# A spectral filter stage with its outer frequencies moved from the free dimension to the partitions

## The chip, the core and the metric

The kernel runs on one core of a Trainium2 chip. The metric is the device time of one execution in microseconds (us), the median of several runs. The profile is one execution of the same program, taken by the hardware profiler.

## The reference

One block of a diffusion-like network over a sequence of 2048 tokens with 640 features, in bf16. A conditioning row `c` gives six modulation vectors (shift, scale and gate for each of two halves). The first half filters the normalised input with a global spectral filter; the second half is a gated feed-forward network.

```python
mod = (silu(c) @ w_mod).reshape(1, 6, 1, 640)
sa, ca, ga, sb, cb, gb = (mod[:, i] for i in range(6))
h = layernorm(x) * (1 + ca) + sa                 # x: (1, 2048, 640)
X = rfft2(h)                                     # (2048, 321) complex
y = irfft2(X * (w_r + 1j * w_i))                 # w_r, w_i: (2048, 321)
x = x + ga * y
h = layernorm(x) * (1 + cb) + sb
x = x + gb * ((silu(h @ w_gate) * (h @ w_up)) @ w_down)   # 640 -> 1728 -> 640
```

Nothing in the reference depends on data: the Fourier transforms can be written as products with constant tables.

## The kernel before

Each token has a number 16 p + t, with p on the 128 partitions and t the tile (16 tiles). The order of instructions on every engine is the order of the calls in the source; each engine (TensorE as PE, VectorE as DVE, ScalarE as ACT, GpSimd as POOL, the DMA queue of SyncE as SP) runs its own in that order and waits on semaphores. Every DMA issued on SP or ACT uses one of eight semaphores in turn, so a DMA is issued only after the one eight places earlier has landed.

**Loads.** SP loads x, the scale columns of w_mod (`wm_ca`), the tables R and G, then (among the last x tiles and the shift columns `wm_sa`) the filter. Two `flip` DMAs (L267) copy w_i and w_r through DRAM into `wflip`, rows reversed; two small edge copies each go on POOL's queue (L261, L263). Two loads (L277) bring the unflipped filter into `Wn`, and two (L426) bring the flipped one from `wflip` into `Wv`; both have the inner row number k1 on the 128 partitions and 256 of the 321 columns. The remaining four column blocks of w_mod (`wm_r`: gate of the first half, then shift, scale and gate of the second) are loaded in two places: the first block ahead of the filter's last loads (L279), the other three behind the transposes (L527, L528).

**Tile loop (L466).** For each tile, PE transposes x (`t1`, L335), ACT copies it (L338), a product with R gives the feature transform (`dfwd`, L315 and L318), DVE corrects it by the mean (`zout`, L382), and `s1` (L393, L394) multiplies with G, scaled on POOL by the reciprocal deviation (`gscale`), for the inner part of the token transform. ACT writes the result to `A_sb` (L397; the last tile in three pieces, L400). The mean and variance of a tile come either from `bn` on DVE (the tiles named in `BN`) or from `gram_stats` (a product on PE and two DVE instructions). Tiles 9 to 15 are handled with reversed token order (`FLIP`). `wsum` (L407) forms w_r + w_i for a three-product complex multiplication, in slices spread over DVE and POOL.

**Filter stage (L516 to L731).** The 321 feature frequencies are four images of 81 base columns l, worked in 21 groups of up to four columns. The first five groups are transposed on PE (`t2_pe`), the others by four DMA transposes (`t2_dma`, L519), so that tile, complex part and residue (16 x 2 x 4) are on the partitions. `stage_a` (L567) multiplies each column, as the weights, with the table KS2: the result in PSUM has the inner frequency k1 on the partitions and 192 outer values (three products x 16 outer frequencies x 4 images) along the free dimension. `prod` (L592) multiplies them with the filter on DVE, 2 instructions of 128x384 per group. `stage_b` (L599) multiplies each of the two halves of the product with the identity: this sums and transposes back, with the outer frequencies on the partitions; ACT copies the result to `Y2` (L602). `stage_c` (L620) applies the inverse outer transform from Ktab; `evac` (L632 to L637) copies two groups at a time to `Em` or `Er`, and `rot` (L648, POOL mostly) writes their rotated copies. The 15 products of `mod_col` (L580, 5 instructions each) for the shift, scale and gate columns of the second half stand near the stage's end. POOL adds the shift's transform `SA` to the transposed columns (`sa_add`, L559).

**The rest.** The inverse transforms (`s1em` L669, `s1er` L678, L1184, L1187), the second normalisation, and the feed-forward network in four chunks follow (L1013, L1043, L891, L914). Its weights are loaded into the filter's buffer once the last filter product is done (`load_gu`, L746).

Of the kernel before, what the change touches and what calls it, by code (L numbers as in the profile page):

```python
# [20 lines left out]
NW = 256  # L21
# [3 lines left out]
BN = (0, 1, 4, 8, 14)  # L25
# [18 lines left out]
def _tables():  # L44
# [39 lines left out]
    KS2 = np.zeros((16, 2, 4, 3, 2, 16, 2))  # L84
    KI = np.zeros((3, 2, 2, 16, 2, 16, 4, 2))
    for m in range(4):
        hl, mm = m // 2, m % 2
        k2 = q if hl == 0 else 15 - q
        F16 = np.exp(-2j * np.pi * np.outer(q, k2) / 16)
        for r in range(4):  # L90
            M = real2(F16 * (-1j) ** (m * r))
            if hl:
                M[:, 1] *= -1
            M = M.transpose(2, 0, 1, 3)
            KS2[:, :, r, 1, hl, :, mm] = M[:, :, 0]
            KS2[:, :, r, 0, hl, :, mm] = -M[:, :, 0] - M[:, :, 1]
            KS2[:, :, r, 2, hl, :, mm] = M[:, :, 1] - M[:, :, 0]
            f = (1.0, 1j ** r, (-1.0) ** r, (-1j) ** r)[m]
            for v in range(3):
                M = real2(F16.conj().T * f * (np.exp(1j * np.pi * r / 4) if v == 2 else 1.0))  # L100
                if hl:
                    M[1] *= -1
                if v >= 1:
                    M[:, 1] *= -1
                KI[v, hl, :, :, mm, :, r, :] = M.transpose(0, 2, 3, 1)
    K = np.zeros((128, 3 * 128 + 192))
    for v in range(3):
        K[:, 128 * v:128 * v + 128] = KI[v].transpose(1, 0, 2, 3, 4, 5, 6).reshape(128, 128)
    K[:, 384:] = KS2.reshape(128, 192)
# [46 lines left out]
def adaln_block_kernel(ctx, tc, A_x, A_w_r, A_w_i, B_x, B_w_gate, B_w_up, B_w_down, c, w_mod, out):  # L156
# [25 lines left out]
    Ktab = const.tile([P, 576], BF16, name="Ktab")  # L182
    KS2 = Ktab[:, 384:576]
# [31 lines left out]
    Wn = rW.cut(0, [3, NT, NW])  # L215
    Wv = rW.cut(24576, [3, NT, NW])
# [39 lines left out]
    dram = ctx.enter_context(tc.tile_pool(name="dram", bufs=1, space=bass.MemoryType.DRAM))  # L256
    Wflip = [dram.tile([P, NT, NW], BF16, name=n) for n in ("wflip_i", "wflip_r")]

    def flip_edge(w, f):
        ncol = w.ap[0][0]  # L260
        nc.gpsimd.dma_start(f[0:1, 0:NT - 1, :], bass.AP(tensor=w.tensor, offset=w.offset + P * ncol + 65,  # L261
                                                        ap=[[P * NT * ncol, 1], [P * ncol, NT - 1], [1, NW]]))
        nc.gpsimd.dma_start(f[0:1, NT - 1, :], w[0:1, 65:65 + NW])  # L263

    def flip(w, f):
        ncol = w.ap[0][0]
        nc.sync.dma_start(f[1:P].rearrange("p k l -> k p l"),  # L267
                          bass.AP(tensor=w.tensor, offset=w.offset + 127 * ncol + 65,
                                  ap=[[P * ncol, NT], [-ncol, P - 1], [1, NW]]))

    nc.sync.dma_start(x_sb[:, 8:12, :], x_v[:, 8:12, :])
    flip(A_w_i, Wflip[0])
    nc.sync.dma_start(x_sb[:, 12:16, :], x_v[:, 12:16, :])  # L273
    flip(A_w_r, Wflip[1])
    nc.sync.dma_start(wm_sa[:], wm_v[:, :, 0:D])  # L275
    for i, w in ((0, A_w_i), (2, A_w_r)):
        nc.sync.dma_start(Wn[:, i, :, :], w.rearrange("(k2 k1) l -> k1 k2 l", k1=P)[:, :, 0:NW])  # L277
    wm_m = wm_v[:, :, 2 * D:6 * D].rearrange("p k (i d) -> p k i d", i=4)
    nc.sync.dma_start(wm_r[:, :, 0, :], wm_m[:, :, 0, :])  # L279
    nc.sync.dma_start(KS2, K_dram[:, 384:576])  # L280
# [44 lines left out]
    if True:  # L325
# [76 lines left out]
        def wsum(W, lo, hi, eng):  # L402

            off = lo if W is Wn else NW - hi
            v = [_rev(W, NT * NW * i + off, [[NW, NT], [160, 2], [1, hi - lo]]) if W is Wn else
                 _rev(W, NT * NW * i + off - 160, [[NW, NT], [160, 2], [1, hi - lo]]) for i in range(3)]
            eng.tensor_tensor(v[1], v[2], v[0], ALU.add)  # L407
# [15 lines left out]
        flip_edge(A_w_i, Wflip[0])  # L423
        flip_edge(A_w_r, Wflip[1])
        for i in range(2):
            nc.sync.dma_start(Wv[:, 2 * i, :, :], Wflip[i][:])  # L426
        nc.sync.dma_start(Ktab[:, 0:384], K_dram[:, 0:384])
# [38 lines left out]
        for t in range(2, NT + 2):  # L466
# [33 lines left out]
            if t in (13, 15):  # L500
                if t == 13:
                    wsum(Wn, 48, 64, nc.vector)
                else:
                    wsum(Wn, 0, 48, nc.vector)
# [7 lines left out]
    if True:  # L512
# [12 lines left out]
        t2_dma(2)  # L525
        t2_dma(3)
        nc.sync.dma_start(wm_r[:, :, 1:3, :], wm_m[:, :, 1:3, :])  # L527
        nc.sync.dma_start(wm_r[:, :, 3, :], wm_m[:, :, 3, :])  # L528
        nc.sync.dma_start(Htab[:], H_dram)
# [23 lines left out]
        def sa_add(g):  # L553
# [3 lines left out]
            if l0 not in seen:  # L557
                seen.add(l0)
                nc.gpsimd.tensor_tensor(B2b[:, :nb, 0:1], B2b[:, :nb, 0:1], SA[:, l0:l0 + nb].unsqueeze(2), ALU.add)  # L559

        def stage_a(g):
            ls = groups[g]
            n = len(ls)
            xps = banks(6 if g == 2 else 2 + 2 * (g % 2), 2, [4, 256])
            for i, l in enumerate(ls):
                B2, j = B2of[l][0:2]
                nc.tensor.matmul(xps[:, i, 0:192], lhsT=B2[:, j, :], rhs=KS2, start=True, stop=True)  # L567
                if i == 0:
                    for c5 in {NG - 4: (0, 1), NG - 3: (0, 1), NG - 2: (2, 3, 4), NG - 1: (2, 3, 4)}.get(g, ()):
                        mod_col(psum[:, 2 + 2 * (g % 2), 192 + c5:193 + c5], wm_r[:, :, 1 + g % 2], c5)  # L570
            PP = rM.cut(1536 * (g % 4), [3, 2, NT, 2, n])
            prod(g, PP, xps, 0)
            if g == 0:
                wsum(Wv, 48, 64, nc.vector)
            prod(g, PP, xps, 1)
# [7 lines left out]
        def prod(g, PP, xps, hl):  # L583
            ls = groups[g]
            n = len(ls)
            xv = xps[:, :n, 0:192].rearrange("p i (v h k m) -> p v h k m i", v=3, h=2, k=NT)
            st = ls[1] - ls[0]
            if hl == 0:
                in1 = _rev(Wn, ls[0], [[NT * NW, 3], [NW, NT], [160, 2], [st, n]])
            else:  # L590
                in1 = _rev(Wv, 255 - ls[0], [[NT * NW, 3], [NW, NT], [-160, 2], [-st, n]])
            nc.vector.tensor_tensor(PP[:, :, hl], xv[:, :, hl], in1, ALU.mult)  # L592

        def stage_b(g, PP):
            n = len(groups[g])
            yps = banks((g + 1) % 2, 1, [4, 128])
            for ps in (1, 0):
                for i in range(n):
                    nc.tensor.matmul(yps[:, i, :], lhsT=_rev(PP, 64 * n * ps + i, [[n, 128]]), rhs=identb[:],  # L599
                                     start=(ps == 1 and i == 0), stop=(ps == 0 and i == n - 1))  # L600
            Y2 = rY.cut(1024 * (g % 4), [4, 128])
            nc.scalar.copy(Y2[:, 0:n, :], yps[:, 0:n, :])  # L602
            return Y2

# [5 lines left out]
        units = [(0, 1), (2, 3), (4,)] + [(g, g + 1) for g in range(5, NG - 2, 2)] + [(NG - 2,), (NG - 1,)]  # L610

        def stage_c(u):
            for g in units[u]:
                ls = groups[g]
                n, l0 = len(ls), ls[0]
                eps_ = banks({NG - 4: 4, NG - 3: 5, NG - 2: 0, NG - 1: 1}.get(g, 6 + (l0 // 4) % 2), 1, [4, 128])
                Y2 = Y2s.pop(g)
                for i, l in enumerate(ls):
                    kv = {0: 1, 80: 2}.get(l, 0)
                    nc.tensor.matmul(eps_[:, i + 4 - n if l0 else i, :], lhsT=Y2[:, i, :], rhs=Ktab[:, 128 * kv:128 * kv + 128],  # L620
                                     start=True, stop=True)

        def evac(u):
            g, l0 = units[u][0], groups[units[u][0]][0]
            if l0 == 0:
                edge = rY.cut(4096, [2, 128])
                nc.scalar.copy(edge[:], banks(6, 1, [4, 128])[:, 0:2, :])
# [3 lines left out]
            elif g == NG - 2:  # L631
                nc.vector.tensor_copy(ep_views(l0, 4), banks(0, 1, [4, 128]).rearrange("p i q -> p q i"))  # L632
            elif g == NG - 1:
                nc.scalar.copy(ep_views(l0, 4), banks(1, 1, [4, 128]).rearrange("p i q -> p q i"))
            else:
                n = len(groups[g]) + 4
                (nc.vector.tensor_copy if g == NG - 6 else nc.scalar.copy)(  # L637
                    ep_views(l0, n), banks(4 if g == NG - 4 else 6, 2, [8, 128])[:, 8 - n:8, :].rearrange("p i q -> p q i"))
                if g < NG - 4:
                    rots.extend((l0, n, i) for i in range(0 if g == NG - 6 else 2))  # L640
# [21 lines left out]
        def s1b(t):  # L662
            return 6 if t == 1 else 2 if t == 0 or t % 2 else 4
# [18 lines left out]
        PPs, Y2s, rots = {}, {}, []  # L682
        ga_mod(320, 5, range(3))
        t2_pe(0)
        t2_pe(1)
        ga_mod(320, 5, range(3, NC5))
        PPs[0] = stage_a(0)
        t2_pe(2)
        t2_pe(3)
        wsum(Wn, 80, 81, nc.gpsimd)  # L690
        PPs[1] = stage_a(1)
        ga_mod(0, 0)
        PPs[2] = stage_a(2)
        for g in range(NG + 1):
# [627 lines left out]
```

## Time and profile before

| | us |
|---|---|
| runs (3) | 249.75, 250.11, 250.72; median 250.11 |
| profiled execution: span from the first to the last instruction | 247.5 (its time outside the span is not on the page) |
| busy in the span: PE / DVE / ACT / POOL | 241.6 / 208.2 / 167.6 / 77.9 |
| filter stage, first transposes to the first L669 product | about 37 to 63 |
| mean DMA rate over the span | 140 GB/s; 281 to 407 GB/s in every 2 us window but one (262) from 4 to 38 us |

In rows of instruction groups the columns are line, engine, operation, output<-input with shapes, count, then busy us and mean ns of one, then the idle time of the engine just before them and what ended it. A line number is that of the kernel before. The granted TensorE clock is 1.00 in every stretch.

### The profile page before, as it was taken

Reading aid. Unit: us, or ns where it says so; the run is one execution under the profiler, and the core shown is the slowest. Engines: PE = TensorE matmul, PEld = TensorE weight load, DVE = VectorE, ACT = ScalarE, POOL = GpSimd, SP = SyncE. Lnnn points to the kernel's source line nnn. Section 1 sums busy time; section 2 is a strip of 40 time slices with the busy share of each in tenths; the row PEclk is TensorE's granted clock in tenths of the full one; section 3 lists DMA queues with packets and bytes.
Section 4 is the critical chain, followed back from the end, with each engine's and each line's share of the span. In section 5 each row is a group of like instructions: output and inputs, shape, how many; then the busy total and the mean of one; then the engine's idle time right before and its main releaser. Section 6 shows DMA issues by size and latency. Waiting matters only on the chain.

```text
span 247.5 us, 6172 instructions
## 1 busy us (share of the span) xinstructions
PE 241.6 (98%) x2327; PEld 189.3 (76%) x2327; DVE 208.2 (84%) x516; ACT 167.6 (68%) x327; POOL 77.9 (31%) x128
## 2 busy tenths in 40 slices
PE   8999998999999999999999999999999999999994
PEld 3778876999999888688887778887765566656773
DVE  4799887998899998789989977788998787789864
ACT  3778756897989698489774488766246777773220
POOL 8577764895243514002004400000432000004400
PEclk9999999999999999999999999999999999999999
DMA  6999999999999999500005110200411000000111
GB/s 211 399 357 301 288 381 219 189 353 390 307 345 304 291 283 191 128 15 3 0 3 106 53 56 3 54 3 19 93 50 53 3 0 1 4 0 0 53 56 53
DMA packets 45759, 34.74 MB, mean 140 GB/s; under 512 B 21731, under 2 KB 42658, under 8 KB 45346
## 3 DMA queue, kind: packets, MB, share of 16 engines
q1 hardware_dynamic: 43936, 30.00, 43.0%
q0 software_dynamic: 1504, 4.28, 7.3%
q8 instruction: 18, 0.29, 0.5%
q10 hardware_dynamic: 290, 0.08, 0.2%
q14 instruction: 11, 0.09, 0.1%
HBM read 27.05 MB, written 4.72 MB: 128 GB/s over the span
## 4 chain that ended last, share of the span: by engine, by line
PE 81%; SPq 10%; DMA 6%; DVE 1%; issue 1%; ACT 0%; DVEq 0%; ACTq 0%
PE psum L1043 36%; PE psum L914 19%; PE psum L1013 6%; DMA rW<-wflip_r 4%; PE psum L599 3%; PE psum L891 3%; PE psum L669 3%; PE psum L567 2%; SPq L273 2%; SPq L277 2%; SPq L275 2%; DMA rM<-in_w_mod_dram 2%; PE psum L620 2%; PE psum L1184 2%; SPq L279 2%; PE psum L1187 2%
## 5 line engine op out<-in xcount | busy, mean ns | idle before, releaser
L1043 PEld LDWEIGHTS <-rW 128*128 128x128 bf16 (+1 forms) x429 | 41.9, 98 | 12.7
L1043 PE MATMUL psum<-rW 128*128 128x256 bf16 (+1 forms) x247 | 42.2, 287 | 0.0
L940 POOL TENSOR_TENSOR rM<-rM,rL 128x320 f32<-128x320 f32 x6 | 5.4, 907 | 96.6 <-ACT rL L939 96.6
L914 PEld LDWEIGHTS <-rE 128*128 128x128 f16 (+1 forms) x196 | 19.0, 97 | 7.8
L914 PE MATMUL psum<-rE 128*128 128x320 f16 (+1 forms) x147 | 22.9, 299 | 0.0
L592 DVE TENSOR_TENSOR rM<-psum,rW 128x384 bf16<-128x384 f32 (+2 forms) x42 | 20.1, 543 | 2.0 <-PE psum L567 1.4
L1074 ACT COPY rH<-psum 128x384 f32<-128x384 f32 (+2 forms) x27 | 13.9, 516 | 7.4 <-PE psum L1043 6.0
L1081 ACT COPY rX<-psum 128x384 f32<-128x384 f32 (+2 forms) x27 | 14.0, 519 | 7.3 <-PE psum L1043 7.0
L1043 PEld LDWEIGHTS <-rE 128*128 128x128 f16 x156 | 15.2, 98 | 4.7
L1078 DVE TENSOR_TENSOR rH<-psum,rM 128x512 bf16<-128x512 f32 (+1 forms) x24 | 15.0, 624 | 4.4 <-PE psum L1043 2.2
L1097 ACT ACTIVATE rL<-psum 128x384 bf16<-128x384 f32 (+2 forms) x27 | 14.4, 532 | 5.3 <-PE psum L1043 3.4
L1082 DVE TENSOR_TENSOR rX<-psum,rX 128x384 f32<-128x384 f32 (+2 forms) x27 | 16.3, 604 | 1.6 <-ACT rX L1081 1.4
L1068 ACT COPY rM<-psum 128x384 f32<-128x384 f32 (+2 forms) x27 | 13.9, 515 | 4.2 <-PE psum L1043 4.2
L382 DVE SCALAR_TENSOR_TENSOR rE<-rE,mv,psum 128x648 bf16<-128x648 f32 (+1 forms) x17 | 14.2, 844 | 2.0 <-PE psum L318 1.5
L1043 PE MATMUL psum<-rE,rY 128*128 128x256 f16 (+1 forms) x78 | 15.6, 290 | 0.0
L1043 PE MATMUL psum<-rW,rE 128*128 128x256 bf16 (+1 forms) x78 | 15.6, 290 | 0.0
L1098 ACT ACTIVATE rL<-rX 128x384 bf16<-128x384 f32 (+2 forms) x27 | 15.1, 558 | 0.0
L338 ACT COPY rE<-psum 128x640 bf16<-128x640 bf16 x16 | 11.1, 694 | 5.7 <-PE psum L336 4.9
L602 ACT CAST rY<-psum 128x512 bf16<-128x512 f32 (+2 forms) x21 | 11.8, 574 | 4.0 <-PE psum L599 3.7
L1013 PE MATMUL psum<-rW 128*128 128x256 bf16 x130 | 14.5, 273 | 0.0
L1189 DVE SCALAR_TENSOR_TENSOR rM<-psum,rX 128x640 f32<-128x640 f32 x16 | 13.1, 820 | 1.6 <-PE psum L1187 1.4
L883 DVE TENSOR_TENSOR rA<-psum,rM 128x320 bf16<-128x320 f32 (+1 forms) x27 | 12.1, 472 | 2.4 <-PE psum L891 2.3
(223 smaller groups left out, 666.1 us busy)
## 6 DMA issues: line engine op xcount, KB each, us to landing
out_dram<-rA SPq DMA_DIRECT2D x31, 80.0 KB, 1.6
rM<-in_w_mod_dram SPq DMA_DIRECT2D x3, 800.0 KB, 10.2
rX<-in_A_x_dram SPq DMA_DIRECT2D x3, 640.0 KB, 7.3
rA<-in_B_w_down_dram SPq DMA_DIRECT2D x2, 960.0 KB, 14.4
rY<-in_B_w_gate_dram POOLq DMA_DIRECT2D x2, 832.0 KB, 7.9
rM<-in_w_mod_dram SPq DMA_DIRECT2D x1, 1600.0 KB, 7.1
rW<-in_B_w_gate_dram SPq DMA_DIRECT2D x2, 640.0 KB, 7.3
rW<-in_B_w_up_dram SPq DMA_DIRECT2D x2, 640.0 KB, 7.1
```

The costliest lines, as they stand in the source:

```text
L382: nc.vector.scalar_tensor_tensor(Zv[:, h], Cv[:, h], mv[:, t, 0:1], zps[:, h], ALU.mult, ALU.subtract)
L592: nc.vector.tensor_tensor(PP[:, :, hl], xv[:, :, hl], in1, ALU.mult)
L914: nc.tensor.matmul(o, lhsT=lhs[rows(k), k], rhs=rhs[rows(k), k], start=start and k == ks[0], stop=stop and k == ks[-1], skip_group_check=True)
L1013: nc.tensor.matmul(gu[u], lhsT=Wgu[:, u, c5, ff * 128:(ff + 1) * 128], rhs=h2T[:, :, c5, :], start=(c5 == 0), stop=(c5 == NC5 - 1))
L1043: nc.tensor.matmul(o[:, f], lhsT=w, rhs=b, start=(start and f == 0 and i == 0), stop=(stop and f == len(groups[g]) - 1 and i == len(ops) - ...
L1068: nc.scalar.copy(c0, X)
L1074: nc.scalar.copy(c2, X)
L1078: nc.vector.tensor_tensor(c11, Z, c0, ALU.add)
L1081: nc.scalar.copy(c3, X)
L1082: nc.vector.tensor_tensor(c22, Y, c3, ALU.add)
L1097: nc.scalar.activation(g21, X, ACT.Silu, scale=-1.0)
L1098: nc.scalar.activation(g22, c22, ACT.Silu, scale=-1.0)
```

## The change

The weights and the moving operand of `stage_a` change places. The table (now 2 x 128 columns of `KX` in Ktab) is the weights, and all columns of a group move through at once: two products of 128x512 per group. The result has the outer frequencies (image pair, complex part, image, k2) on the 128 partitions and (column, inner frequency k1) along the free dimension. Two versions v, the value and its complex partner, are multiplied with w_r and w_i as they are, which makes an ordinary complex product of two terms; `wsum` goes. `stage_c` takes the two products as weights directly and sums them in PSUM with a table that has the signs in it, so `stage_b` with its identity products and `Y2` copies goes.

The filter is loaded once, in the layout of that product (`Wt`): 16 outer rows x 128 inner rows x 161 columns into 16 partitions, for w_r and w_i and two column halves (64 partitions), with eight small loads for the wrapped edge row. The flipped half is written to partitions 64 to 127 by `w_rev` on DVE, four copies that read rows and columns backwards, at t = 13 to 16 of the tile loop. Flips, `Wn` and `Wv` go.

In eleven groups (`MIX`) ACT copies the second version to SBUF, DVE multiplies the first and POOL the second; in the other ten DVE multiplies both in one instruction. `stage_c` and its evacuation go group by group, mostly on ACT. Five rotations and the four `sa_add` go from POOL to DVE. All four blocks of `wm_r` are loaded ahead of the transposes, and the `mod_col` products stand behind the third `stage_a`; Htab is loaded ahead of the last transpose. Tile 6 instead of 14 takes its statistics from `bn`: tile 14, whose token order is reversed, gets them from `gram_stats`, in that order.

```diff
-NW = 256
+RW = 164
-BN = (0, 1, 4, 8, 14)
+BN = (0, 1, 4, 6, 8)
...
-    Wn = rW.cut(0, [3, NT, NW])
-    Wv = rW.cut(24576, [3, NT, NW])
+    Wt = rW.cut(0, [P + 1, RW])
+    Ktab = rW.cut(42496, [1024])
...
+    def load_w(w, c):
+        ncol = w.ap[0][0]
+        for mm in range(2):
+            h = Wt[32 * c + 16 * mm:32 * c + 16 * mm + 16]
+            nc.sync.dma_start(h[:, 0:P, 0:161], bass.AP(tensor=w.tensor, offset=w.offset + 160 * mm,
+                                                       ap=[[P * ncol, NT], [ncol, P], [1, 161]]))
...
     nc.sync.dma_start(x_sb[:, 8:12, :], x_v[:, 8:12, :])
-    flip(A_w_i, Wflip[0])
+    load_w(A_w_r, 0)
     nc.sync.dma_start(x_sb[:, 12:16, :], x_v[:, 12:16, :])
-    flip(A_w_r, Wflip[1])
     nc.sync.dma_start(wm_sa[:], wm_v[:, :, 0:D])
-    for i, w in ((0, A_w_i), (2, A_w_r)):
-        nc.sync.dma_start(Wn[:, i, :, :], w.rearrange("(k2 k1) l -> k1 k2 l", k1=P)[:, :, 0:NW])
+    load_w(A_w_i, 1)
+    load_edge(A_w_r, 0)
+    load_edge(A_w_i, 1)
+    nc.sync.dma_start(Ktab[:], K_dram)
-    nc.sync.dma_start(wm_r[:, :, 0, :], wm_m[:, :, 0, :])
-    nc.sync.dma_start(KS2, K_dram[:, 384:576])
+    for i in range(4):
+        nc.sync.dma_start(wm_r[:, :, i, :], wm_m[:, :, i, :])
...
+        def w_rev(k, n):
+            src = Wt[0:64]
+            nc.vector.tensor_copy(Wt[64:P, k:k + n, 0:82],
+                                  bass.AP(tensor=src.tensor, offset=src.offset + (P - k) * RW + 160,
+                                          ap=[list(src.ap[0]), [-RW, n], [-1, 82]]))
...
-            if t in (13, 15):
-                if t == 13:
-                    wsum(Wn, 48, 64, nc.vector)
-                else:
-                    wsum(Wn, 0, 48, nc.vector)
+            if 13 <= t <= NT:
+                w_rev(26 * (t - 13), 26 if t < NT else 50)
...
         def stage_a(g):
...
+            for v in range(2):
+                nc.tensor.matmul(xps[:, v], lhsT=Ktab[:, 128 * v:128 * v + 128], rhs=B2[:, j:j + n, :].rearrange("p l k -> p (l k)"),
+                                 start=True, stop=True)
...
+            if g in MIX:
+                Xs = rY.cut(1024 * (g % 3), [P, n])
+                nc.scalar.copy(Xs[:], xv[:, 1])
+                nc.vector.tensor_tensor(PP[:, 0], xv[:, 0], wv[:, 0], ALU.mult)
+                nc.gpsimd.tensor_tensor(PP[:, 1], Xs[:], wv[:, 1], ALU.mult)
+            else:
+                nc.vector.tensor_tensor(PP[:], xv, wv, ALU.mult)
...
+        def stage_c(g):
...
+            for i, l in enumerate(ls):
+                kv = {0: 1, 80: 2}.get(l, 0)
+                for v in range(2):
+                    k0 = 256 + 128 * (2 * kv + v)
+                    nc.tensor.matmul(eps_[:, i, :], lhsT=_rev(PP, P * n * v + i, [[n, P]]), rhs=Ktab[:, k0:k0 + 128],
+                                     start=(v == 0), stop=(v == 1))
...
+        PPs[2] = stage_a(2)
+        for i, j in enumerate((1, 2, 3)):
+            for c5 in range(NC5):
+                mod_col(psum[:, 0, 5 * i + c5:5 * i + c5 + 1], wm_r[:, :, j], c5)
...
+        for g in range(1, NG + 2):
+            sa_add(g + 3)
+            if g + 2 < NG:
+                PPs[g + 2] = stage_a(g + 2)
...
+            if g > 1:
+                stage_c(g - 2)
```

## Prediction

> **What bounds the kernel now.** I read the windows first (busy time by stretch). PE is busy for 10.0 of every 10 us from 60 us on (60 to 70: 9.98) until the closing stores; of the 5.9 us it idles in the 247.5, 3.4 lie in the last stretch. So whatever moves the moment at which PE leaves the filter stage moves the end by as much. That moment is the first L669 product, at 63.0 us. The chain of waits then says what led to it:
>
> ```profile
> 28.52 1.08 SPq L280
> 29.73 0.35 SPq L426
> 30.26 9.08 DMA rW<-wflip_r
> 39.43 0.44 DVE rW L407
> ```
>
> Columns: start, length, what. Up to 39.3 us the chain is SP's queue and the filter's way through DRAM; after it, PE's groups. Who waited on that landing, and for how long, is in VectorE's timeline:
>
> ```profile
> 32.16 0.89 DVE L382 SCALAR_TENSOR_TENSOR rE<-rE,mv,psum 128x648 bf16<-128x648 f32 x1
> 32.97 0.42 DVE L407 TENSOR_TENSOR rW<-rW 128x512 bf16<-128x512 bf16 x1
> ...
> 33.91 1.85 DVE L382 SCALAR_TENSOR_TENSOR rE<-rE,mv,psum 128x648 bf16<-128x648 f32 x3
> 35.68 0.95 DVE L407 TENSOR_TENSOR rW<-rW 128x1536 bf16<-128x1536 bf16 x1
> 37.11 0.49 DVE L542 TENSOR_TENSOR rM<-psum,gb_bc 128x256 bf16<-128x256 bf16 x2 [0.48 <-ACT rA L400]
> 38.03 0.56 DVE L592 TENSOR_TENSOR rM<-psum,rW 128x384 bf16<-128x384 f32 x1 [0.43 <-PE psum L567]
> 39.43 0.43 DVE L407 TENSOR_TENSOR rW<-rW 128x512 bf16<-128x512 bf16 x1 [0.83 <-DMA rW<-wflip_r]
> ```
>
> The late filter costs VectorE only 0.83 us. For the rest the stage (37 to 63 us) is a balance of four busy engines. From its groups (count, busy us, mean ns, idle before):
>
> ```profile
> L592 DVE TENSOR_TENSOR rM<-psum,rW 128x384 bf16<-128x384 f32 (+2 forms) x42 | 20.1, 543 | 2.0 <-PE psum L567 1.4 <-issue 0.4
> L637 DVE CAST rE<-psum 128x1024 bf16<-128x1024 f32 x1 | 1.2, 1212 | 0.0
> L632 DVE CAST rE<-psum 128x512 bf16<-128x512 f32 x1 | 0.7, 683 | 0.0
> L648 DVE TENSOR_SCALAR rE<-rE 128x512 bf16<-128x512 bf16 x2 | 0.5, 296 | 0.0
> ...
> L648 POOL TENSOR_SCALAR rE<-rE 128x512 bf16<-128x512 bf16 (+1 forms) x14 | 8.3, 611 | 2.4 <-ACT rE L637 2.4
> ...
> L602 ACT CAST rY<-psum 128x512 bf16<-128x512 f32 (+2 forms) x21 | 11.8, 574 | 4.0 <-PE psum L599 3.7
> ...
> L407 POOL TENSOR_TENSOR rW<-rW 128x512 bf16<-128x512 bf16 x5 | 5.7, 1157 | 0.0
> ```
>
> Last the DMA side: the best of the 2 us windows (last columns: busy share of the DMA engines, GB/s), and from the page a queue (packets, MB, share of 16 engines' span).
>
> ```profile
> 6.00:8.00 2.00, 2.00 (x34) 1.31 (x32) 0.91 (x5) 0.99 (x4) 1.06 (x2) 1.00 1.09 407
> ...
> q10 hardware_dynamic: 290, 0.08, 0.2%
> ```
>
> The other windows from 4 to 39 us show the DMA engines as full (0.96 to 1.20), so a load that gets slower there finds no gap to hide in.
>
> **The filter loads.** Removed: two 1 MB flips through DRAM, their edges on POOL's queue (four issues near 0.52 us at 5 us, landed long before use), two 1 MB loads of Wn and two of Wv, 6.1 MB. Added: four loads of 16 partitions x 128 rows x 322 B (0.66 MB each) and eight small edge loads. The bytes fall by more than half, but each load writes 16 partitions instead of 128, in pieces of 322 B. The trace has no such load, so I bound one, D us, from both sides. Low: the q10 row holds 256 pieces of that size (128 of 324 B from table R, 128 of 320 B in the last store): 0.2% of 16 x 247.5 us over 290 packets is 27 ns each (20 to 34 with the rounding). A load has 128 packets per engine: D = 3.5 (2.6 to 4.4). High: the best window, 407 GB/s over 128 partitions, gives a partition 3.2 GB/s; at that rate the 41.2 KB that each partition receives take D = 13. Neither row is near in both respects, so I take the geometric middle: 6.7 from 3.5, 5.8 from 2.6; D = 6.3.
>
> [...]
>
> When do they land? The windows to 12 us sum to 3.65 MB, so the 3.6 MB queued in front (x tiles 0 to 11, the scale columns of w_mod, tables R and G) are through at 11.8. Then 2D; x tiles 12 to 15 and the shift columns of w_mod, 1.48 MB at 350 GB/s (the windows from 14 to 18 show 377 and 342), 4.2; 2D; an estimated 1.0 to land. In the changed order each SP transfer waits for the one eight places earlier, so the last two edge loads wait for the last two filter loads; issue and landing 1.7 (an 80 KB store lands in 1.6). Filter complete at 18.7 + 4D = 43.9 us.
>
> **What waits for it.** The first reversed copy of w_rev reads the edge row, so it needs all twelve loads, and it stands on VectorE behind zout(13), which ended at 32.97. VectorE stops there for 43.9 - 32.97 = **10.9 us**; behind it are zout(14), zout(15), the SA vectors and every product, so PE's s1(14) and s1(15), ScalarE's copies and the transposes stop too. x tiles 12 to 15 land at 27.3; tile 12's transposes (L335) began at 23.10: 4.2 us for the tile loop, inside the 10.9.
>
> **The copies.** w_rev: three of 26 x 82 elements, one of 50 x 82. Low: L648 on DVE, one bf16 source in SBUF, 0.296 at 512 with some 0.15 fixed (a 5-element copy): 0.7 and 1.25, with overlap. High: L632 to L637, 1.03 ns per element: 2.35 and 4.4. No DVE row reads backwards; I take the low pair as the nearest kind, 3.35 in all. wsum's 0.42 and 0.95 go. From 32.97: 0.7, SA 0.33, zout 0.85, 0.7, zout 1.0, 0.7, 1.25 ends at 38.5, where L542 began at 37.11: **+1.4**.
>
> [...]
>
> **The stage itself.** DVE: nine full groups of 128x1024 at 1.21, eleven products of 128x512 at 0.68, one of 384 at 0.54, seven rotations near 0.28, four sa_adds near 0.16, L542 0.5, one evacuation 0.68: 22.8 against 23.7. ACT: the Y2 copies (11.8) and paired evacuations (8.1) give way to eleven Xs copies and nineteen evacuations near 0.58: about -1.8. PE by start spacing: 81 columns x (0.083 + 0.112 + 0.056) = 20.3 becomes 42 products at 0.22 less the short groups and 162 at 0.056: 18.0, -2.3. POOL: 18.4 becomes eleven 128x512 products near 1.16 (12.5), nine rotations (5.5) and small ones (2.4): 20.4, **+2.0**, in order, and stage_c waits for half its products there. Bounds -2.3 and +2.0; I take **-1.3**, nearer the low end, since stage_a runs two groups ahead of stage_c and so hides most of a late product.
>
> **The moved w_mod columns.** All four parts (3.3 MB) with Ktab now stand ahead of the transposes on SP. They can be issued only once the last filter load has landed (42.2): + 0.8 + 3.54 MB at 360 GB/s, 9.8, + 1.0 = 53.8. The 75 mod_col products moved from the stage's end to behind stage_a(2), which PE reaches at 52.0 (38.5 + 0.5 + 10.9 and 2.1 for three groups, transposes and ga_mod). PE waits 1.8, stage_a(3) is queued behind, and VectorE has only three products to live on; the first transpose lands some 3.5 us after the columns, about when group 5 asks: **+1.9**. With filter loads in time the columns land near 42 and this is nearly covered.
>
> Edits at nothing: tile 6 takes the bn statistics and tile 14 the gram ones (the same instructions; PE's extra 0.45 us at t = 12 stands ahead of PE's wait at 33.05). Htab now precedes the last transpose, which is read only by the four last groups. load_gu waits for the last product and lands in about 7; its first reader came 17 us later; without that cover, a few us more.
>
> **Sum.** 10.9 + 1.4 - 1.3 + 1.9 = +12.9. The profiled execution spans 247.5; the page gives no time of its own beside the span, and the median of the three runs, 250.1, is 2.6 above it, which I leave unchanged: **263.0 us**. Own range, D from 5 to 7.3: 257 to 268.
>
> **Rivals.** (A) The loads run at the packet rate, D up to 3.6, filter complete before 33.0, no stop. Then the stage decides: with POOL's products on the path, 1.4 - 1.3, 250.2; if PE's and ACT's lighter sums end it, -2.3 with the +1.4 under PE's head start of two groups, 247.8, faster. For it: the 20 to 34 ns packets and 3.5 MB less traffic. Against it: never in this trace do 16 engines write 16 partitions. From D = 3.6 on every further 0.1 costs 0.4 us. (B) The reversed copies run one element per cycle, 11.4 for 3.35: +8.0, 258 with loads in time, 271 otherwise. (C) The partition rate holds fully, D = 13: +27 more, 290. That the identity products do not disappear is excluded: the changed instruction order has none.
>
> **How the numbers follow.** Forecast and its neighbours 257 to 268: 0.60. Between 251.4 and 257 (D near 4 to 5, or B alone at its shorter end): 0.07. A without gain: 0.10; A with gain: 0.18. B on top, or C: 0.05. About 0.5% (1.25 us) is what a measurement of this kernel tells from no change; the three runs spread 0.4%. So faster 0.18, same 0.10, slower 0.72. The range 248 to 268 leaves out the better half of A's gain (about 0.10) and the tail above (0.05 to 0.08).
>
> **What would show it.** Right: in the profile after, the first reversed copy on VectorE waits for a filter or edge DMA until about 44 us, near 11 us of idle; PE has a gap of that length before 45, and a second one at mod_col for w_mod. The 26-row copies take 0.6 to 0.8 us. POOL carries eleven products near 1.16. Wrong: a first copy that starts at 33 without a wait, or filter loads that take under 4 us; a first copy of 2.3 us speaks for B.

## The result, and the profile after

The changed kernel takes 284.58 us (median of 4 runs, 283.28 to 285.61) against 250.29 (249.75 to 250.72): a ratio of 1.138, interval 1.134 to 1.143. The forecast of 263.0 and its range to 268 were too low; direction and kind of wait were as forecast. The profiled execution took 283.28 us with a span of 281.5, 34.0 longer than before.

Where they went is read from two timelines of the kernel after (start, length, engine, line, operation, in brackets idle time and what ended it). VectorE first:

```profile
48.98 0.88 DVE L383 SCALAR_TENSOR_TENSOR rE<-rE,mv,psum 128x648 bf16<-128x648 f32 x1
61.71 0.72 DVE L405 COPY rW<-rW 64x2132 bf16<-64x2132 bf16 x1 [11.86 <-DMA rW<-in_A_w_i_dram]
...
65.41 1.89 DVE L405 COPY rW<-rW 64x2132 bf16<-64x2132 bf16 x2
68.81 0.49 DVE L532 TENSOR_TENSOR rM<-psum,gb_bc 128x256 bf16<-128x256 bf16 x2 [1.52 <-issue]
```

The first reversed copy starts at 61.71, on the landing of w_i. Before, that place in VectorE's order (behind zout(13)) was reached at 32.97. L532 is the stage's first instruction, L542 before, at 37.11. TensorE shows a second stop, ahead of the transposes of tile 12, then the waits in the filter stage and the start of the first inverse product:

```profile
36.78 0.61 PE L336 MATMUL psum<-identb,rX 128*128 128x128 bf16 x4 [13.85 <-DMA rX<-in_A_x_dram]
...
79.88 0.59 PE L557 MATMUL psum<-rL,rW 128*128 128x512 bf16 x2 [0.95 <-DVE rL L549]
85.09 0.59 PE L557 MATMUL psum<-rL,rW 128*128 128x512 bf16 x2 [1.66 <-DVE rL L549]
90.29 0.59 PE L557 MATMUL psum<-rM,rW 128*128 128x512 bf16 x2 [1.52 <-DVE rM L549]
...
96.93 1.06 PE L633 MATMUL psum<-rH,rE 128*128 128x128 bf16 x16
```

That product before:

```profile
63.03 1.28 PE L669 MATMUL psum<-rH,rE 128*128 128x128 bf16 x20
```

So the 34.0 us divide into the stop up to the first reversed copy (61.71 - 32.97 = 28.7), from there to L532 (7.10 against 4.14: +3.0), the stage to L633 (28.12 against 25.92: +2.2), and the rest (184.57 against 184.47: +0.1). What the DMA engines did in the stop is in the windows (last three columns: granted TensorE clock, DMA share, GB/s):

```profile
14.00:16.00 2.00, 1.74 (x18) 1.16 (x15) 1.97 (x10) 1.42 (x3) 1.64 (x5) 1.00 1.40 57
26.00:28.00 2.00, 0.00 (x0) 0.00 (x0) 0.00 (x0) 0.00 (x0) 0.00 (x0) 0.50 1.41 60
34.00:36.00 2.00, 0.00 (x0) 0.00 (x0) 0.00 (x0) 0.00 (x0) 0.00 (x0) 0.50 0.94 285
40.00:42.00 2.00, 2.00 (x16) 1.64 (x15) 1.26 (x4) 0.69 (x1) 1.49 (x4) 0.50 1.40 61
```

While filter loads run, the DMA engines count as more than full and move 57 to 61 GB/s in the rows shown (55 to 89 in the other windows of these loads, where other transfers are among them). The x tiles behind the first pair go at 285 (34 to 36). At 61 GB/s a load of 0.66 MB takes D = 10.8 us. SyncE's queue says the same: its last edge load, eight places behind the last filter load, was issued only when that had landed (the queue's wait for w_i: 8.5 us) and stands at

```profile
60.44 0.22 SPq L269 DMA_DIRECT2D rW<-in_A_w_i_dram  x1
```

and the prediction's sum puts that place at 17.0 + 4D, so D = 10.9. The window rows also show the clock: 0.50 while TensorE stands idle (26 to 28 and 34 to 36 us), and still 0.50 from 40 to 42, when it works again.

The stage's groups after (count, busy us, mean ns, idle before) answer to those shown of before:

```profile
L570 DVE TENSOR_TENSOR rM<-psum,rW 128x1024 bf16<-128x1024 f32 (+1 forms) x9 | 10.8, 1203 | 1.2 <-PE psum L557 1.2
L567 DVE TENSOR_TENSOR rM<-psum,rW 128x512 bf16<-128x512 f32 (+1 forms) x9 | 5.9, 669 | 0.2 <-PE psum L557 0.2
L612 DVE TENSOR_SCALAR rE<-rE 128x512 bf16<-128x512 bf16 (+2 forms) x9 | 5.0, 576 | 0.0
L549 DVE TENSOR_TENSOR rL<-rL,SA 128x16 bf16<-128x16 bf16 (+1 forms) x3 | 2.5, 829 | 0.0
...
L568 POOL TENSOR_TENSOR rM<-rY,rW 128x512 bf16<-128x512 bf16 (+1 forms) x9 | 10.3, 1158 | 1.9 <-ACT rY L566 1.7
```

Products and GpSimd's durations are as priced. The rotations on VectorE (L612, 576 ns mean, priced near 280) and the sa_adds (L549, 829, priced 160) are not.

### The profile page after: what moved, and what is told of

Read it like the earlier page. It is cut to its first block, busy times and chain, and to the rows that moved or that the text cites. A ratio compares the mean times of both kernels' runs of the same rounds, so it can differ in the third digit from the quotient of the medians.

```text
span 281.5 us, 5891 instructions
## 1 busy us (share of the span) xinstructions
PE 243.9 (87%) x2207; PEld 186.1 (66%) x2207; DVE 212.9 (76%) x501; ACT 165.2 (59%) x330; POOL 78.0 (28%) x119
## 4 chain that ended last, share of the span: by engine, by line
PE 67%; DVE 3%; issue 0%; ACT 0%; DVEq 0%
PE psum L998 32%; PE psum L869 17%; PE psum L968 5%; PE psum L846 3%; PE psum L633 2%; PE psum L557 2%; PE psum L1139 2%; PE psum L1142 2%; PE psum L956 2%; PE psum L592 1%; DVE rM L570 1%; DVE rE L612 1%; PE psum L642 1%; DVE rL L549 0%; ACT rL L637 0%
## 5 line engine op out<-in xcount | busy, mean ns | idle before, releaser
L394 PE MATMUL psum<-rE 128*128 128x324 bf16 (+1 forms) x34 | 11.1, 341 | 12.2 <-DVE SA L479 12.2
L398 ACT CAST rA<-psum 128x648 bf16<-128x648 f32 x15 | 10.5, 700 | 18.7 <-PE psum L395 18.2
L336 PE MATMUL psum<-identb,rX 128*128 128x128 bf16 x64 | 6.9, 236 | 14.2 <-DMA rX<-in_A_x_dram 13.9
L336 PEld LDWEIGHTS <-rX 128*128 128x128 bf16 x64 | 5.3, 120 | 16.2 <-DMA rX<-in_A_x_dram 14.9
L363 DVE SCALAR_TENSOR_TENSOR rE<-psum,identb 128x128 bf16<-128x128 f32 x11 | 3.1, 284 | 15.6 <-PE psum L361 15.5
## 6 DMA issues: line engine op xcount, KB each, us to landing
rW<-in_A_w_r_dram SPq DMA_DIRECT2D x2, 644.0 KB, 19.9
```

The lines of the kernel that those rows point to most:

```text
L336: nc.tensor.transpose(xt[:, r, :], xr[:, r, :], identb[:])
```

## The experiments

Each ran once beside one run of the kernel before on the same chip, and times are given as differences to that. The kernel before itself took 248.84 to 250.97 there, both on one chip, so two differences can lie 2 us apart for no reason in the change, and the argument goes by the last columns. They are places in the timeline: the first reversed copy, L532, and the stage from there to L633. Differences in brackets are of kernels with plain copies for the DMA transposes and are not compared.

| run | us, before there | difference | first copy | L532 | stage |
|---|---|---|---|---|---|
| after, profiled | 283.28, 250.29 | +33.0 (medians +34.3) | 61.71 | 68.81 | 28.1 |
| e1_spread | 254.02, 248.84 | +5.2 | 33.33 | 39.60 | 28.1 |
| e2_long | 264.91, 248.84 | +16.1 | 43.63 | 50.39 | 28.1 |
| e3_every2nd | 266.61, 248.84 | +17.8 | 43.34 | 51.32 | 28.9 |
| e15_every4th | 262.74, 248.96 | (+13.8) | 41.59 | 48.24 | |
| e5_xfirst | 286.52, 250.97 | +35.6 | 61.49 | 68.36 | 31.8 |
| e4_saadd_pool | 288.54, 248.84 | +39.7 | 62.36 | 70.35 | 31.8 |
| e6_noproduct | 251.85, 250.97 | +0.9 | 33.47 | 39.73 | 25.5 |
| e9_rot_act | 253.60, 249.62 | +4.0 | 33.17 | 39.43 | 27.6 |
| e7_twoqueues | 264.02, 250.97 | +13.1 | 41.03 | 47.72 | 29.9 |
| c1 | 272.18, 249.62 | +22.6 | 57.51 | 59.08 | 26.6 |
| e14_bank | 254.89, 248.96 | (+5.9) | 33.46 | 39.05 | |
| e8_tile6 | 250.26, 250.97 | -0.7 | | | |

### What makes the filter loads slow: e1_spread, e2_long, e3_every2nd, e15_every4th

e1_spread: the same number of pieces, over all partitions.

```diff
-            h = Wt[32 * c + 16 * mm:32 * c + 16 * mm + 16]
-            nc.sync.dma_start(h[:, 0:P, 0:161], ... offset=w.offset + 160 * mm, ap=[[P * ncol, NT], [ncol, P], [1, 161]]))
+            j = 2 * c + mm
+            nc.sync.dma_start(Wt[:, 16 * j:16 * j + 16, 0:164], ... offset=w.offset + 157 * mm, ap=[[16 * ncol, P], [ncol, 16], [1, 164]]))
...
-            wv = _rev(Wt, ls[0], [[0, 2], [RW, P], [st, n]])
+            wv = _rev(Wt, ls[0], [[0, 2], [RW // 2, P], [st, n]])
```

(w_rev reads at half the row pitch likewise.)

> Left out: the filter's places. Each of the four loads writes 16 pieces of 328 B to each of 128 partitions (not 128 pieces to each of 16), and products and reversed copies read the buffer with half the row pitch, so the filter values that meet a frequency are not the reference's; the number and nearly the size of the pieces, and every instruction's element count, stay. Theory W (the few partitions that a load writes set its time): D falls from 10.5 to at most 3.7 us (0.67 MB at 180 GB/s or more), the filter lands before 33 us, no stop of PE and VectorE: 252 us (250 to 257). Theory P (pieces this small cost some 110 ns each wherever they go): D stays near 10.5 and the time at 284 (281 to 287). It also shows the filter stage with its loads in time: 28 us if its length comes from the engines, 24.6 (my -1.3) if the late loads lengthened it.

e2_long: the same partitions, one run each.

```diff
-            nc.sync.dma_start(h[:, 0:P, 0:161], ... ap=[[P * ncol, NT], [ncol, P], [1, 161]]))
+            nc.sync.dma_start(h[:, 0:P, :].rearrange("p a b -> p (a b)"), ... ap=[[P * ncol, NT], [1, P * RW]]))
```

> Left out: the rows' places. Each of the 16 partitions of a load takes one unbroken run of 41,984 B instead of 128 pieces of 322 B, so rows of the filter don't lie where the products look for them; bytes, partitions and everything else stay. Theory W: the piece doesn't matter, D stays near 10.5, 284 us (280 to 287). Theory P: with long pieces D falls to 6.3 us or below, the filter lands near 44 or earlier: 252 to 268 us. If both act, D ends between 6.3 and 10: 268 to 281 us.

e3_every2nd and e15_every4th: 16 partitions per load, farther apart; KX and KI permuted alike.

```diff
-            h = Wt[32 * c + 16 * mm:32 * c + 16 * mm + 16]
+            h = Wt[32 * c + mm:32 * c + 32:2]     # e3_every2nd
+            h = Wt[2 * c + mm:64:4]               # e15_every4th
```

> The whole reference. The partitions of the filter's two column halves are interleaved (a load writes every second of 32 partitions, 16 in all), and the rows of the tables that go with them are permuted alike. Theory W by the number of partitions: 16 as before, D 10.5, 284 us (281 to 287). [...] Theory P: 284.

> Left out: the turning of rows into columns in all nine DMA transposes, which are plain copies of the same blocks here, so only the loads and waits ahead of the filter stage can be compared. Partition order with the inner two bits for component and column half: a load writes every fourth of 64 partitions, 16 in all; the tables are permuted alike. [...] If it is the spread over groups of four partitions that counts, they are 16 groups: 200 GB/s or more, D near 3, the first reversed copy at 33 to 34 without a wait.

The window from 14 to 16 us of e3_every2nd, e1_spread and e15_every4th, in this order:

```profile
14.00:16.00 2.00, 1.82 (x21) 1.40 (x19) 1.93 (x10) 1.42 (x3) 1.74 (x4) 1.00 1.40 115
```

```profile
14.00:16.00 2.00, 1.82 (x21) 1.40 (x19) 1.93 (x10) 1.42 (x3) 1.74 (x4) 1.00 1.16 249
```

```profile
14.00:16.00 2.00, 1.82 (x21) 1.40 (x19) 1.93 (x10) 1.42 (x3) 1.74 (x4) 1.00 1.39 120
```

57 GB/s became 115 when the same 16 partitions were every second of 32, and stayed near that (120) when they were every fourth of 64, although they then touch twice as many groups of four neighbours. Over 128 partitions it is 249. The first reversed copies of e2_long, e3_every2nd and e15_every4th:

```profile
43.63 0.72 DVE L405 COPY rW<-rW 64x2132 bf16<-64x2132 bf16 x1 [4.64 <-DMA rW<-in_A_w_i_dram]
```

```profile
43.34 0.72 DVE L405 COPY rW<-rW 64x2132 bf16<-64x2132 bf16 x1 [4.87 <-DMA rW<-in_A_w_i_dram]
```

```profile
41.59 0.72 DVE L405 COPY rW<-rW 64x2132 bf16<-64x2132 bf16 x1 [4.91 <-DMA rW<-in_A_w_i_dram]
```

For e3_every2nd I had also reckoned with half of D, 5.2 us, and 263 us (257 to 270): it took 266.61. e15_every4th started 1.75 us ahead of it (41.59 against 43.34), far from the 33 to 34 of 16 groups. Neither theory holds alone. Few partitions with long runs (e2_long): by the prediction's 18.7 + 4D = 43.63, an estimated D of 6.2, 0.67 MB at 108 GB/s. Short pieces over all partitions (e1_spread): 249 GB/s, so the landing is in time. Both together: 61. The rates of the 322 to 328 B pieces double and double again (57 to 61, 115 to 120, 249). Estimated from these rates, the 2048 pieces of a load take 10.8 us in the kernel after, 5.7 in e3_every2nd (0.66 MB at 115 GB/s) and 2.7 in e1_spread (0.67 MB at 249 GB/s). Why every second and every fourth partition came out alike, and where the limit for neighbouring partitions comes from, no run shows. That pieces of 322 B lose on the same partitions is shown (61 against the estimated 108 GB/s of e2_long), not at which size the loss begins.

### Does the wait for x add to it: e5_xfirst

```diff
-    load_w(A_w_r, 0)
     nc.sync.dma_start(x_sb[:, 12:16, :], x_v[:, 12:16, :])
     nc.sync.dma_start(wm_sa[:], wm_v[:, :, 0:D])
+    load_w(A_w_r, 0)
     load_w(A_w_i, 1)
```

> The whole reference. x tiles 12 to 15 and the shift columns of w_mod are issued ahead of the first two filter loads instead of behind them. Theory F (only the landing of the last filter load sets the end; the 13.85 us that TensorE waits for x in the kernel after is time that it would spend at the filter's wait otherwise): the wait for x goes, the first reversed copy waits 25 us instead of 11.9 and starts at 61 to 63 us as before; 282 to 286 us. Theory X (the wait for x adds to the filter's): 270 to 274.

```profile
61.49 0.72 DVE L405 COPY rW<-rW 64x2132 bf16<-64x2132 bf16 x1 [28.43 <-DMA rW<-in_A_w_i_dram]
```

The 13.85 us of TensorE's wait are gone, and the filter's wait is 28.43 instead of 11.86: theory F. The landing of the last filter load alone sets the start. The time is half a microsecond above theory F's range, for another reason that VectorE's timeline shows further on:

```profile
76.54 0.23 DVE L549 TENSOR_TENSOR rL<-rL,SA 128x15 bf16<-128x15 bf16 x1 [1.59 <-DMA rL<-rA]
```

The first DMA transpose, queued behind the w_mod columns, came late here; TensorE waited 1.72 us behind it, its clock was 0.53 and 0.62 in the windows from 76 to 80 and again 0.80, 0.50 and 0.85 from 92 to 98, and the stage took 31.8 us. In the kernel after the same addition ran at 75.31 without a wait.

### What the stage costs: e4_saadd_pool, e6_noproduct, e9_rot_act

In e1_spread the filter lands in time and the stage still takes 28.1 us, as in the kernel after: its extra time is its own. e4_saadd_pool:

```diff
-                nc.vector.tensor_tensor(B2b[:, :nb, 0:1], B2b[:, :nb, 0:1], SA[:, l0:l0 + nb].unsqueeze(2), ALU.add)
+                nc.gpsimd.tensor_tensor(B2b[:, :nb, 0:1], B2b[:, :nb, 0:1], SA[:, l0:l0 + nb].unsqueeze(2), ALU.add)
```

> The whole reference. The four additions of SA to the transposed columns go back from VectorE to GpSimd, nothing else. Theory L (VectorE's instruction with two operands in SBUF waits for the product that runs on GpSimd): in the kernel after they took 0.21, 1.10, 1.17 and 0.63 us and TensorE waited 0.95 to 1.66 us for three of them; on GpSimd they stand in order behind the same products, so TensorE waits as long for them or longer: stage 28.1 us (27 to 30), time 283 to 286. Theory M (they are merely misplaced on a busy VectorE): stage 26 to 27, time 281 to 283.

It got worse, beyond theory L's range: stage 31.8. Not all of that is the additions'. Some 0.7 is before them: the clock stood at 0.50 up to 72 us, and the second GpSimd product began 7.48 us behind L532 instead of 6.77. And behind the first addition the clock fell once more, to 0.80, 0.50 and 0.85 in the windows from 78 to 84 us, while it stayed at 1.00 in the stage of the kernel after. The additions are short on GpSimd (0.27 to 0.34 us), but stand behind its products and rotations, and TensorE waits for all four (1.48, 1.68, 1.28, 1.11 us). So the run gives no sign that their move to VectorE was a mistake; how the 3.7 us divide between waits and clock it doesn't show. e6_noproduct, on e1_spread:

```diff
-                Xs = rY.cut(1024 * (g % 3), [P, n])
-                nc.scalar.copy(Xs[:], xv[:, 1])
+                nc.scalar.copy(PP[:, 1], xv[:, 1])
                 nc.vector.tensor_tensor(PP[:, 0], xv[:, 0], wv[:, 0], ALU.mult)
-                nc.gpsimd.tensor_tensor(PP[:, 1], Xs[:], wv[:, 1], ALU.mult)
```

> Built on e1_spread (the filter in time, in other places). Left out besides: the product of the second version with the filter in the eleven groups of MIX; ScalarE's copy writes straight to where GpSimd's product wrote, so GpSimd does nothing there. Theory L (VectorE's instructions that read only SBUF wait for GpSimd's): the sa_adds, mean 0.78 us in e1_spread, take near 0.2 each, the 128x512 rotations on VectorE, up to 1.24, near 0.3, TensorE no longer waits at the sa_adds, and the stage falls from 28.1 to 24 to 25.5 us: 3 us less than e1_spread, 249.5 to 251.5. Theory M (VectorE is the bound by its products and evacuation): the durations stay and the stage loses under 1 us: 253 to 254.

Its VectorE timeline:

```profile
51.10 0.22 DVE L549 TENSOR_TENSOR rL<-rL,SA 128x16 bf16<-128x16 bf16 x1
...
58.71 0.28 DVE L610 TENSOR_SCALAR rE<-rE 128x512 bf16<-128x512 bf16 x1
```

The stage falls to 25.5, and the two instructions take 0.22 and 0.28 where they were priced at 0.16 and 0.28: theory L by durations and stage, though the time lies 0.35 us above its range. The kernel after shows the overlap itself. VectorE's line, then GpSimd's, twice:

```profile
78.72 1.10 DVE L549 TENSOR_TENSOR rL<-rL,SA 128x16 bf16<-128x16 bf16 x1
88.42 1.26 DVE L612 TENSOR_SCALAR rE<-rE 128x512 bf16<-128x512 bf16 x1
```

```profile
78.58 1.15 POOL L568 TENSOR_TENSOR rM<-rY,rW 128x512 bf16<-128x512 bf16 x1 [0.27 <-ACT rY L566]
88.35 1.18 POOL L568 TENSOR_TENSOR rY<-rY,rW 128x512 bf16<-128x512 bf16 x1
```

Each VectorE instruction began just behind a GpSimd product and ended 0.09 and 0.15 us after its end. The sa_add at 75.31, with GpSimd idle until 75.58, took 0.21. The products that VectorE reads from PSUM keep their 0.68 beside GpSimd; an sa_add and a rotation took 0.22 and 0.28 without GpSimd's products (e6_noproduct). What in the hardware holds up those that read only SBUF, no run shows.

e9_rot_act, on e1_spread, moves the rotations only:

```diff
-                rot(l0, n, slice(0, 64), nc.vector if (l0, n, i) in DROT else nc.gpsimd, (i,))
+                rot(l0, n, slice(0, 64), nc.scalar if (l0, n, i) in DROT else nc.gpsimd, (i,))
...
+                if eng is nc.scalar:
+                    eng.mul(E1[:, :, 1 - i, :], E0[:, :, i, :], 1.0 - 2.0 * i)
```

> Built on e1_spread (the filter in time, in other places). The five rotations of DROT go from VectorE to ScalarE, the sa_adds stay on VectorE. If the stage's 2.5 us that e6_noproduct took away came from VectorE's waits for GpSimd as a whole, the five rotations (4.2 us busy in e1_spread) are the larger part: the stage falls from 28.1 to 26 to 27, TensorE's waits at the sa_adds shrink because VectorE reaches them earlier, and the time is 1 to 2 us under e1_spread's on the same chip (e1_spread was 5.2 above before there: so 3 to 4 above before). If only the sa_adds count, since TensorE waits for those alone, nothing changes (within 0.5 us).

The stage is 27.6, only 0.45 shorter than in e1_spread, and the span 0.4 (251.8 against 252.2), which by the expectation speaks for the sa_adds alone. But the clock differs: it was 1.00 through the stage in e1_spread, and fell behind mod_col in the other two, to 0.86, 0.50 and 0.79 (e6_noproduct) and 0.75, 0.50 and 0.89 (e9_rot_act) in the windows from 44 to 50 us. The timelines separate this. VectorE's product ahead of the second sa_add began 9.31 us behind L532 in e1_spread, 10.78 in e6_noproduct and 10.77 in e9_rot_act, 1.5 later in both. From there to the first inverse product they took 18.75, 14.75 and 16.84 us. So leaving out GpSimd's products saved 4.0 us behind that place, not 2.5, and moving the rotations 1.9, which is what was expected of them. In e9_rot_act TensorE's longest wait at a sa_add fell from 1.65 to 0.96 us, but TensorE now waits for ScalarE's evacuations (0.34, 0.53, 0.18), which stand behind the rotations. How the other 2.1 of the 4.0 us divide between the sa_adds and stage_c's waits for late GpSimd products is not settled, and why the clock fell in these runs is not shown.

### Smaller terms: e14_bank, e8_tile6

```diff
-        ga_mod(320, 7)
+        ga_mod(320, 5)
```

> Built on e1_spread (the filter in time, in other places). Left out besides: the turning of rows into columns in all nine DMA transposes, which are plain copies of the same blocks here, so only the time up to the first stage_a of group 5 can be compared. The first half of ga_mod writes to PSUM bank 5 instead of bank 7, which s1 of the last tile holds until ScalarE has copied it. If the 0.7 us that VectorE idles ahead of L532 in e1_spread come from that (ga_mod waited 0.91 us for ScalarE, and the transposes on TensorE stand behind it), L532 starts at 38.9 to 39.1 us, where the reversed copies end at 38.9, instead of 39.6. If the transposes wait for ScalarE's copy anyway, it starts at 39.4 or later.

L532 follows the last reversed copy at 39.05, without the idle 0.69. The moved ga_mod had a cost that I had not seen: bank 7 belongs to the last tile's s1 until ScalarE has copied it.

```diff
-BN = (0, 1, 4, 8, 14)
+BN = (0, 1, 4, 6, 8)
```

> The kernel before with one part of the change alone: tile 6 instead of tile 14 takes its statistics from bn, tile 14 from gram_stats. The prediction costed it at nothing: within 0.4% of the kernel before on the same chip, 247.9 to 249.9 if that is 248.84. The rival: gram_stats of tile 14 puts 5 products and two VectorE instructions into the last tiles of the loop, where TensorE's groups follow one another, 0.5 to 1 us slower.

0.3% under the run of before beside it, within what can be told from no change: no cost of that edit shows.

### Can the loads be hidden: e7_twoqueues, c1

e7_twoqueues, on e3_every2nd (w_i's loads stay on SyncE, behind x and wm_sa):

```diff
+    nc.scalar.activation(warm[:], warm[:], ACT.Silu)
+    load_w(A_w_r, 0, nc.scalar)
     for xl, xh, gl, gh in ((2, 4, 0, 2), (4, 8, 2, NG9)):
...
-    load_w(A_w_r, 0)
     nc.sync.dma_start(x_sb[:, 12:16, :], x_v[:, 12:16, :])
```

> The whole reference. [...] If packets of the filter hold the DMA engines themselves, x comes late in the first 15 us: the tile loop stalls by 5 us or more, 258 to 265.

The first copy waits only 0.36 us, but the whole tile loop is late: ScalarE stood 8.43 us ahead of its first silu, by the profile for an x transfer (the second w_r load, which stands ahead of the silu, was issued only at 11.00), and in the window from 6 to 8 us the DMA engines moved 148 GB/s at a share of 1.23. For queues that run beside each other without a stop I had reckoned with 252 to 256 us; the 264.02 measured is in the recorded range of 258 to 265. Whether x came late or the second issue was held is not separated here. The stage of 29.9 has a lowered clock in it (0.77, 0.50, 0.50 and 0.53 from 52 to 60 us), behind waits for the w_mod columns and the first transpose. c1 keeps the partition order of e3_every2nd and moves all four loads to ScalarE, later, and the edge loads to GpSimd's queue; Ktab and three of the four w_mod blocks are issued behind the filter, and the rotations of DROT stand on ScalarE:

```diff
+        load_w(A_w_r, 0, 0)          # ScalarE's queue, behind t1(0)
+        load_w(A_w_r, 0, 1)
...
+        load_w(A_w_i, 1, 0)          # behind t1(2)
+        load_w(A_w_i, 1, 1)
...
-            if 13 <= t <= NT:
-                w_rev(26 * (t - 13), 26 if t < NT else 50)
+            if t == NT:
+                w_rev(48, 64)        # by columns; (64, 82) and (20, 48) between the first products
+                w_rev(0, 20)
...
+        ga_mod(320, 5)
```

> The whole reference, the version that the runs point to. [...]

I had forecast 249.5 to 253 us, with the loads running beside x and the filter complete at 32 to 37. It took 272.18, and what failed was the first assumption. ScalarE's timeline:

```profile
17.63 0.69 ACT L331 COPY rE<-psum 128x640 bf16<-128x640 bf16 x1 [0.90 <-PE psum L329]
17.64 12.85 ACTq L259 DMA_DIRECT2D rW<-in_A_w_i_dram  x2
```

Issuing the two w_i loads occupied ScalarE for 12.85 us (the w_r pair 9.01), and its copies for the tile loop stood behind. The semaphores that these two wait for are those of G and x tiles 4 to 7, issued by 5.1 us, and such transfers landed 6.6 (G) and 7.1 us (x) after their issue in this run, so by 17.64 they were free: no semaphore explains the hold. SyncE's queue in the kernel after shows the same, where no compute stands behind it, and in e2_long, with one run per partition, these loads' issue takes 0.32 to 0.58 us:

```profile
25.13 14.78 SPq L260 DMA_DIRECT2D rW<-in_A_w_i_dram  x2
```

```profile
L260 SPq DMA_DIRECT2D rW<-in_A_w_i_dram x2: 320/448/577, 8.1 to 10.0; - x2
```

The hold is not the price of one load. In the kernel after the first w_r load was issued in 0.71 us and the second in 7.64, and an edge load of 15 pieces behind the last filter load was held 9.73:

```profile
39.95 9.73 SPq L267 DMA_DIRECT2D rW<-in_A_w_r_dram  x1
```

In e1_spread, where the pieces move at 249 GB/s, the pairs took 6.65 and 5.59 us, against 8.39 and 14.78 in the kernel after. What limits the queue, no run shows.

From the reversed copies on, c1 did what it was made for (copies end at 59.07, L532's counterpart starts at 59.08, stage 26.6), but its tile loop ended 22 us late. No version of this change that was run beats the kernel before.

## Why the prediction was wrong

**The step that failed is D, the time of one filter load.** I bounded it by 3.5 us (short pieces at 27 ns, spread over all 16 engines) and 13 us (a partition rate) and took 6.3, between the two geometric middles 6.7 and 5.8, as if one limit or the other would act. D measured 10.8, outside the 5 to 7.3 of the likeliest case; the upper bound of 13 held. The runs show that both limits act on the same load: long pieces on the same 16 partitions go at an estimated 108 GB/s, short ones over 128 partitions at 249, short ones on 16 neighbouring partitions at 57 to 61. My 6.3 came near the estimated 6.2 of e2_long, the load with long pieces, not the load that the change makes.

**The formula around it was right.** 18.7 + 4D with the measured D = 10.8 gives 61.9; the copy started at 61.71. With D = 5.7 to 6.0 (the 110 to 115 GB/s of e3_every2nd's windows) it gives 41.5 to 42.7; that copy started at 43.34. With the measured stop of 28.7 and the forecast's other terms unchanged, the sum is 28.7 + 1.4 - 1.3 + 1.9 = +30.7, 280.8 us.

**x inside the filter's wait: right** (e5_xfirst), at 13.85 instead of 4.2 us.

**The copies: right.** 0.72 each for 26 rows, 1.89 for the last two; rival B is out. From first copy to L532 before's 4.14 became 5.59 in e14_bank, which is the forecast's +1.4. The rest of the +3.0 is ga_mod's bank, 0.7 (6.27 in e1_spread, at a clock of 1.00), and about 0.8 of lowered clock (7.10 in the kernel after; 7.98 and 7.99 in e3_every2nd and e4_saadd_pool, where the clock stayed at 0.50 up to L532). That 0.8 is a comparison of runs, not an experiment of its own.

**The stage: wrong sign**, +2.2 for -1.3, just outside the bound of +2.0. Four sa_adds were priced at 0.16 and five rotations at 0.28, as if GpSimd's products beside them cost VectorE nothing; they took 0.21 to 1.17 and up to 1.26. No run shows the forecast's 24.6: without GpSimd's products the stage took 25.5, of which some 1.5 is lowered clock, so an estimated 24.0 with nothing in the way, but that kernel also lacks the products themselves. (ScalarE's -1.8 is -2.5 by its own terms, 19.9 against 30 x 0.58; no bound rests on it.)

**The w_mod columns: +1.9 did not appear, but was near.** They were issued at 61.18, and mod_col ran at 72.41 without a wait; between the first copy and mod_col the slow clock and the longer way to L532 had left time for them. In e5_xfirst the transposes behind them were late by 1.59 us, and in e7_twoqueues, with a shorter way to mod_col, ga_mod waited 1.27 and mod_col 0.44 us for them. Htab, load_gu and the later phases moved one for one (+0.1).

**Rivals.** A (loads in time) was excluded by D, though e1_spread shows what it would have been: a span of 252.2, 4.7 above the 247.5 of before, not +0.1 or -2.3. Of the 4.7, 2.5 are up to L532 (copies and ga_mod's bank) and 2.1 the stage. C (D = 13, 290) was the nearest; at 0.05 shared with B it had too little of the chance.

## What to carry to other kernels

When a load has two handicaps, small pieces and few partitions close together, expect both at once: here the loss from each came on top of the other (an estimated 108 and 249 GB/s alone, 57 to 61 together), and a middle between two single limits was no estimate. A change of layout for the compute side should be priced as a DMA first, and taking 16 partitions that are every second one of 32 nearly halved the load here (an estimated 5.7 us for 10.8) for a permuted table. Before work goes from GpSimd to VectorE, look at whether it reads only SBUF: beside GpSimd's products such instructions took up to 1.26 us here instead of 0.21 to 0.28. When two runs are compared by a stage's length, compare the granted clock in it first: in e9_rot_act it hid three quarters of the gain.

## What the runs showed that was not expected

DMAs of 2048 short pieces held the engine that issued them, and what was issued behind them: 12.85 us for two on ScalarE (c1), 14.78 on SyncE (the kernel after), while one with 16 long runs took 0.32 to 0.58 (e2_long). In c1 a second queue on a computing engine was no way to hide such loads.

In the kernel after, TensorE's granted clock fell in the idle stretches (0.91 from 24 to 26 us, 0.50 from 26 to 36) and stayed low into the work behind them: 0.50 for all of 36 to 42 us, 0.83 from 42 to 44. The reversed copy, with negative steps in rows and columns, ran 2132 elements in 0.72 us and 4100 in 1.24: 0.26 ns for each further element, where the PSUM evacuations behind the prediction's high price take 1.03.
